# Three versions of the expert stage behind one branch on the token counts, in a fused attention, expert and feed-forward kernel

## The chip, the core and the metric

One core of a Trainium2 chip runs the whole program in one launch. The metric is device time in microseconds (us), the median over executions. TensorE (PE in the rows, PEld its weight loads), VectorE (DVE), ScalarE (ACT), GpSimd (POOL) and SyncE (SP) each work through a queue of their own, in order; a letter q behind an engine's name (PEldq, POOLq) marks what its sequencer does alone: register loads, branches, semaphores.

## The reference, cut to what matters

```python
# attention: q, k, v of 4 x 8 x 576 x 64; a row keeps its 32 largest scores, softmax, times v
x = attn_out as (2304, 512)
expert_idx = argmax(normalised x @ normalised expert_emb.T / tau)     # 8 experts
for e in range(8):                                                    # each token goes to one expert
    mask = expert_idx == e
    out[mask] = gate_w[mask] * (relu(x[mask] @ w1[e]) @ w2[e])        # 512 -> 1024 -> 512
h = out @ w_in                                                        # 512 -> 2048
return (max(h, 0) + alpha * min(h, 0)) @ w_out                        # 2048 -> 512
```

How many tokens an expert gets is known only when the router has run. The inputs are drawn by the reference itself with its default seed.

## The kernel before, in words

The program has three stages: attention with the router in its gaps, the expert stage, and the feed-forward stage (`last_products`). The router sorts tokens by expert into a DRAM buffer `xs` and ranks the experts: rank 0 is the expert that led after three of four batches, ranks 1 to 7 follow by size. The expert stage cannot have loops of a length found at run time, so each rank is computed over a fixed number of columns (tokens), `CAPS = (472, 408, 360, 328, 304, 296, 280, 256)`; columns beyond the expert's count are filled with rows that are thrown away. Two flags (`ro.flag`, L847 to L851) tell that a count went over its cap; in that case a branch at the end (L1842) redoes the rest, or all of it, in slow general code.

`Experts.run` (L1157) writes the stage out. It goes over nine blocks of columns: rank 0 in two (216 and 256 columns, blocks 0 and 1), then ranks 1 to 7 in one each (blocks 2 to 8). A block has two halves. In the first half each of 8 hidden tiles `f` takes 4 x 3 matmuls of n columns (L1108 to L1110: the numbers are split in a high and a low part, and three products are added), then ACT writes the high part (L1203) and DVE the low part (L1204). In the second half each of 4 output chunks `dc` takes 8 x 3 matmuls, and ACT or DVE copies it out of PSUM to `y` (L1246, L1248), from where SP stores it to the DRAM buffer `yt` (L1249). So a block is 192 matmuls of n columns. Between the chunks PE turns the next block's rows (`x_chunk`, L1100, one transpose for each 96 to 128 rows and each of 4 chunks). Weights come 8 units of 512 KB for an expert; SP fetches them (L921) into four buffers `raw`, and ACT and DVE or POOL split each in two halves (L1032, L1033) into one of 12 places. `tick` hands out these steps, and those of the feed-forward weights, by the list `plan`: a rank's first four units are split in the first half of the block before, its other four in the second half. Each engine's queue is in the order of the program text.

The feed-forward stage follows at the same pace on PE, then the last indirect stores of POOL (L1369), then every engine loads the flag word `redo` (L1840) and branches over the general code (L1842); each waits at semaphores that stand for what the skipped code would have counted.

Names that the steps below use: `ranks` (L816), `flags` and `redo` (L1140, L1149; a PE matmul L1152 sums the flags over partitions), `load_rows` (L1067), `load_columns` (L1260), `plan` (L1166), `stores` (L1249).

Of the kernel before, what the change touches and what calls it, by code (L numbers as in the profile page):

```python
# [502 lines left out]
CAPS = (472, 408, 360, 328, 304, 296, 280, 256)  # L503
FIRST = 216
XW = DM + 2
AHEAD = 3
# [10 lines left out]
class Router:  # L517
# [298 lines left out]
    def ranks(self):  # L816
# [6 lines left out]
        rank, first, t1 = self.rev, self.base, gt  # L823
        self.excess, self.over = key, gt[:, 0, 0:1]
        r3 = lambda a: a[:, None, :].to_broadcast([P, E, E])
        c3 = lambda a: a[:, :, None].to_broadcast([P, E, E])
# [25 lines left out]


def wide_words(nc, wk, raw, bufs):


    n = raw.shape[1] // 2
    v = raw.rearrange("p (f w) -> p f w", w=2)
    low, high = v[:, :, 0], v[:, :, 1]
    a = wk.tile([P, n], I32, name="wa", bufs=bufs)  # L860
    nc.vector.tensor_scalar(a, high, 3, 0x3FFFFFF8, op0=OP.logical_shift_left, op1=OP.bitwise_and)
    nc.vector.scalar_tensor_tensor(a, high, -0x40000000, a, op0=OP.bitwise_and, op1=OP.bitwise_or)
    nc.vector.tensor_scalar(high, a, -0x800000, None, op0=OP.bitwise_and)
# [5 lines left out]
SLOTS, EARLY, STAY = 12, 6, 8  # L869

LASTS = (0, 1, 2, 3, 8, 9, 10, 11, 4, 5, 6, 7, 12, 13, 14, 15)
# [14 lines left out]
class Experts:  # L886
# [3 lines left out]
    def __init__(self, tc, w1, w2, w_in, w_out, wa, xp, ident, xs, yt, idc, yp, ro, out):  # L890
        self.tc, self.nc = tc, tc.nc
        self.w1, self.w2, self.w_in, self.w_out = w1, w2, w_in, w_out
        self.ident, self.xs, self.yt, self.idc, self.out = ident, xs, yt, idc, out
        self.ro, self.wa, self.xp, self.yp = ro, wa, xp, yp
        self.W, self.rv = {}, {}
        self.items, self.sent = [], 0
        self.h0, self.p0, self.behind, self.ahead_of = [], [], [], []
        self.columns, self.numbers = None, []

# [23 lines left out]
    def unit(self, k):  # L923
        pool, n = (self.wa, EARLY) if k % SLOTS < EARLY else (self.wb, SLOTS - EARLY)
        return pool.tile([P, 2, 1024], F32R, name="wt", bufs=n)

# [23 lines left out]
    def plain(self, k):  # L950
        st = {}

        def load():
            st["r"] = self.wk.tile([P, 1024], F32, name="raw", bufs=4)
            self.fetch(st["r"], k)
        return load, lambda: self.split(k, st["r"])

    def wide(self, u, i):


        st, nc = {}, self.nc
        cs = slice(i * 512, (i + 1) * 512)

        def load():
            st["r"] = self.wk.tile([P, 1024], I32, name="raw", bufs=4)
# [42 lines left out]
    def first_blocks(self):  # L1008

        raws, v, nothing = {}, self.nc.vector, lambda: None  # L1010

        def add(j, m):
            def f():
                if not raws:
                    raws.update((i, self.wk.tile([P, 4, G2], F32, name="raw", bufs=4)) for i in (5, 6, 7, 4))
                self.sums(raws.get)[j][1]()
            return f
# [49 lines left out]
    def load_rows(self, r, o, n):  # L1067
# [4 lines left out]
        e, base = self.rv[r]  # L1072
        x = self.xp.tile([P, 4, XW], F32, name="xr")
        ld = nc.sync.dma_start(x[:p, :nj], self.xs[ds(e * NT + o, p * nj)].rearrange("(j p) d -> p j d", p=p))
# [19 lines left out]
    def x_chunk(self, rows, n, d, pt=None):  # L1094
# [4 lines left out]
        for j in range(nj):  # L1099
            nc.tensor.transpose(pt[:, j * p:(j + 1) * p], x[:p, j, d * P:(d + 1) * P], self.ident[:p, :p])  # L1100
        t = self.xp.tile([P, 2, MAXN], F32R, name="xT", bufs=4)
        nc.scalar.activation(t[:, 0, :n], pt[:, :n], AF.Copy)
# [46 lines left out]
    def redo(self, ones, f):  # L1149
# [4 lines left out]
        nc.vector.tensor_copy(n, pt[:, 0:2])  # L1154
        nc.vector.scalar_tensor_tensor(self.ro.redo, n[:, 0:1], 256.0, n[:, 1:2], op0=OP.mult, op1=OP.add)

    def run(self, ctx, alpha):  # L1157
# [9 lines left out]
        for r in range(1, E):  # L1167
            plan += [units(r + 1, 0), units(r + 1, 1)]
        blocks_of, none = self.first_blocks()
        plan[-2] += [self.last(d) for d in range(4)]  # L1170
# [13 lines left out]
        self.send(4)  # L1184
        rki = self.ro.rki
        ranks = self.ro.ranks()
# [4 lines left out]
        self.alpha = self.wk.tile([P, FF2 // P], F32, name="alpha")  # L1191
        nc.sync.dma_start(self.alpha, alpha.rearrange("(f p) -> p f", p=P))
        xT = self.x0
        for i, (r, o, n) in enumerate(blocks):
            nb = blocks[i + 1] if i + 1 < len(blocks) else None
            hT, nx = ([] if i else self.h0), []
            self.n = len(plan[2 * i])
            for f in range(8):
# [8 lines left out]
                if i == 0:  # L1207
# [4 lines left out]
                    if len(ranks) < 14 and 1 not in self.rv:  # L1212
                        registers()
                        rows = [self.load_rows(*nb)]
                if f >= GAT and nb and i:
                    self.gate(rows[0], f - GAT)
# [4 lines left out]
            if not nb:  # L1221
                nx = self.halves(rows[0])
            if i == 1:
                fl = self.flags()
            if i == 2:
                self.redo(*fl)
            base = self.rv[r][1]
            self.n = len(plan[2 * i + 1])

            def turn(at):  # L1230
                if nb:
                    nx.extend([self.x_chunk(rows[0], nb[2], d) for d in (XAT if i else XAT0)[at]])
# [24 lines left out]
            xT, rows = nx, rows[1:]  # L1257
        self.last_products(xT, len(plan[-2]), len(plan[-1]))

    def load_columns(self, g):  # L1260

        x = self.columns
        if x is None:
            x = self.columns = self.xp.tile([P, 4, XW], F32, name="xr")
        if g * G2 < NT:
# [8 lines left out]
    def halves(self, x):  # L1274
        out = []
        for d in range(4):
            t = self.xp.tile([P, 2, MAXN], F32R, name="xT", bufs=4)
            self.nc.scalar.activation(t[:, 0, :G2], x[:, d, :G2], AF.Copy)
# [4 lines left out]
    def last_products(self, t, n0, n1):  # L1283
# [133 lines left out]
        def new_sum(j):  # L1417
            if not raws:
                raws.update((i, self.wk.tile([P, 4, G2], F32, name="raw", bufs=4)) for i in (5, 6, 4, 7))
            self.sums(raws.get)[j][1]()  # L1420
# [75 lines left out]
        for m in (1, 6, 7, 5, 4, 2, 3):  # L1496
            product(k, m)


# [263 lines left out]
def tile_kernel(ctx, tc, q, k, v, emb, tau, w1, w2, w_in, w_out, alpha, out):  # L1763
# [11 lines left out]
    with ExitStack() as c0:  # L1775
# [95 lines left out]
```

## Time and profile before

| what | value |
|---|---|
| median of 3 runs (lowest, highest) | 1115.79 us (1114.88, 1116.54) |
| the profiled execution: its time | 1116.8 us |
| the profiled execution: its span, first to last instruction | 1115.1 us |
| mean granted TensorE clock | 0.998 |
| busy: PE, DVE, POOL, ACT | 96%, 78%, 67%, 65% |
| attention and router, up to the first matmul of rank 0's second block | 486.9 us |
| expert stage from there on (blocks 1 to 8) | 227.5 us |
| feed-forward stage, to the end of the span | 400.7 us |

The sum of a change is made against the profiled execution, which stands 1.0 us above the median of the runs; the 1.7 us between its time and its span lie around the first and last instruction. A stage is read from the stretch that it takes, since the shares of the whole span mix stages with different limits.

### The profile page before, as it was taken

What the parts mean: (1) busy time and instruction counts of PE and PEld (TensorE: products, weight loads), DVE (VectorE), ACT (ScalarE), POOL (GpSimd) and SP (SyncE); (2) the same over time, 40 slices, a digit from 0 to 9 for tenths busy, and PEclk for the clock granted to TensorE, in tenths of its full rate; (3) what the DMA queues carried; (4) which work ended last, traced back from release to release, by engine and by line L of the source; (5) the groups of instructions that cost most, each with busy time, mean ns of one, the idle gap of its engine ahead of it and who ended that gap; (6) DMA issues with size and microseconds to landing.
All of it is one profiled execution on the core that took longest, in us unless ns stands there. A gap on an engine that the chain in (4) does not pass through costs nothing. (4 is left out here: it accounts for less than half of the span.)

```text
span 1115.1 us, 27488 instructions
## 1 busy us (share of the span) xinstructions
PE 1068.7 (96%) x9529; PEld 1016.9 (91%) x9529; DVE 871.0 (78%) x3441; ACT 727.8 (65%) x1549; POOL 750.5 (67%) x790
## 2 busy tenths in 40 slices
PE   6999999999999998999999999999999999999996
PEld 4888889888887887999999999999999999999996
DVE  6999999999999999745456567787899978466554
ACT  6999999999999989645345555453434355433441
POOL 6999988888988888424435444255656695664674
PEclk9999999999999999999999999999999999999999
DMA  7456333443343324267567777146646122212301
GB/s 180 130 150 153 96 94 99 108 124 99 90 114 99 67 53 174 61 205 249 195 207 225 222 244 232 39 86 111 101 115 139 39 63 78 90 57 67 124 21 41
DMA packets 149531, 134.99 MB, mean 121 GB/s; under 512 B 95054, under 2 KB 117582, under 8 KB 149382
## 3 DMA queue, kind: packets, MB, share of 16 engines
q1 hardware_dynamic: 145334, 123.01, 41.0%
q0 software_dynamic: 2912, 9.46, 2.3%
q8 instruction: 77, 1.26, 0.5%
q10 hardware_dynamic: 1136, 0.67, 0.2%
q14 instruction: 72, 0.59, 0.2%
HBM read 89.82 MB, written 33.92 MB: 111 GB/s over the span
## 5 line engine op out<-in xcount | busy, mean ns | idle before, releaser
L1108 PE MATMUL mm<-xT,wt 128*128 128x256 f32 (+7 forms) x852 | 245.8, 288 | 2.1 <-DVE y L1382 2.1
L1109 PE MATMUL mm<-xT,wt 128*128 128x256 f32 (+7 forms) x852 | 246.3, 289 | 0.8 <-DVE xT L1279 0.8
L1110 PE MATMUL mm<-xT,wt 128*128 128x256 f32 (+7 forms) x852 | 245.5, 288 | 0.0
L297 POOL TENSOR_TENSOR sg<-ss,sg 128x576 f32<-128x576 f32 x143 | 201.7, 1412 | 32.0 <-ACT sg L286 30.2
L211 DVE MAX8 cand<-ss 128x8 f32<-128x96 f32 x864 | 210.8, 245 | 8.2 <-ACT ss L201 7.5
L1381 PE MATMUL mm<-wt,hT 128*128 128x256 f32 x1512 | 193.6, 282 | 1.1 <-DVE y L1382 0.9
L1381 PEld LDWEIGHTS mm<-wt,hT 128*128 128x128 f32 x1512 | 184.9, 189 | 2.2 <-issue 1.1
L1108 PEld LDWEIGHTS mm<-xT,wt 128*128 128x128 f32 x852 | 160.7, 189 | 3.0 <-DVE y L1382 2.7
L1109 PEld LDWEIGHTS mm<-xT,wt 128*128 128x128 f32 x852 | 160.8, 189 | 1.2 <-DVE xT L1279 1.2
L1110 PEld LDWEIGHTS mm<-xT,wt 128*128 128x128 f32 x852 | 160.9, 189 | 0.0
L970 POOL TENSOR_TENSOR wf<-wa,raw 128x512 f32<-128x512 f32 x32 | 48.8, 1524 | 117.2 <-DVE raw L865 83.2
L286 ACT ACTIVATE sg<-ss,w 128x576 f32<-128x576 f32 x144 | 118.3, 822 | 4.6 <-DVE w L224 4.0
L291 ACT ACTIVATE e<-ss,sm 128x576 f32<-128x576 f32 x144 | 117.6, 817 | 0.0
L322 PE MATMUL pt<-ident,e 128*128 128x128 f32 x576 | 114.9, 280 | 0.3 <-ACT pT L342 0.2
L323 PE MATMUL pt<-away,pen 128*128 128x128 bf16 x576 | 106.0, 220 | 2.7 <-POOL pen L306 2.7
L1033 POOL TENSOR_TENSOR wt<-raw,wt 128x1024 fp32r<-128x1024 f32 x28 | 68.5, 2447 | 58.5 <-ACT wt L1032 58.3
L233 DVE MAX8 w<-sg 128x8 f32<-128x576 f32 x144 | 106.5, 740 | 0.0
L189 PE MATMUL s<-kt,qq 64*128 64x144 f32 (+1 forms) x1280 | 100.3, 310 | 5.4 <-ACT pb L345 2.3
L201 ACT ACTIVATE ss<-s 128x576 f32<-128x576 f32 x144 | 100.2, 696 | 5.1 <-PE s L189 3.0
L189 PEld LDWEIGHTS s<-kt,qq 64*128 64x128 f32 (+1 forms) x1280 | 78.9, 183 | 22.1 <-issue 7.7
L356 PE MATMUL po<-va,pT 128*128 128x65 f32 (+1 forms) x640 | 86.6, 278 | 8.1 <-ACT pc L391 8.1
L342 ACT ACTIVATE pT<-pt 128x512 f32<-128x512 f32 x144 | 91.8, 637 | 0.8 <-PE pt L323 0.8
(295 smaller groups left out, 2731.2 us busy)
## 6 DMA issues: line engine op xcount, KB each, us to landing
raw<-in_moe_w SPq DMA_DIRECT2D x59, 512.0 KB
xr<-yt SPq DMA_DIRECT2D x17, 512.0 KB
qq<-qt SPq DMA_DIRECT2D x60, 144.0 KB
xs<-zeros SPq DMA_DIRECT2D x8, 1028.0 KB
raw<-in_moe_w_in SPq DMA_DIRECT2D x16, 512.0 KB
raw<-in_moe_w_out SPq DMA_DIRECT2D x16, 512.0 KB
yt<-zeros SPq DMA_DIRECT2D x8, 704.0 KB
rows<-in_q SPq DMA_DIRECT2D x32, 144.0 KB
```

The costliest lines, as they stand in the source:

```text
L189: nc.tensor.matmul(s[to, g, c * n:c * n + n], t["qq"][of, h, q0:q0 + m], t["k"][of, h * HALF + c * n:h * HALF + c * n + n], start=True, st ...
L211: blocks.append(lambda i=i: nc.vector.max(A.cand[:, i], A.ss[:, i * BW:(i + 1) * BW if i + 1 < KB else S]))
L233: fin = [lambda: nc.vector.max(C.w[:, 24:32], C.z), lambda: nc.vector.scalar_tensor_tensor(scr, self.vsel, C.c1, C.w[:, 23:32, None].to_br ...
L286: nc.scalar.activation(T.sg, T.ss, AF.Sign, bias=T.w[:, 23:24], scale=-ABOVE, accum_out=T.c1)
L291: nc.scalar.activation(T.e[:, self.place(T)], T.ss, AF.Exp, bias=T.sm[:, 0:1], scale=0.125)
L297: eng.tensor_tensor(T.z, T.ss, T.sg, op=OP.mult)
L322: nc.tensor.matmul(o, T.e[:, k:k + P], self.ident, is_transpose=True, start=True, stop=False)
L323: nc.tensor.matmul(o, T.pen[:, k:k + P], self.away, start=False, stop=True)
L1108: nc.tensor.matmul(ps, wh, xh, start=first, stop=False)
L1109: nc.tensor.matmul(ps, wh, xl, start=False, stop=False)
L1110: nc.tensor.matmul(ps, wl, xh, start=False, stop=last)
L1381: nc.tensor.matmul(ps, a[:, x, c], b[:, y, c], start=c == r == 0, stop=c == 3 and r == 2)
```

## The change

Block 1 is the last that all versions share. Behind it a branch on a word `wider`, which DVE computes from the counts, chooses among three versions of blocks 2 to 8 and of the whole feed-forward stage, which differ in the columns for ranks 1 to 7. The first version listed under the branch is `FLAT` or, by a second branch, `CAPS`; `STEEP` stands last. Python writes all that follows three times, from the same state. Tiles that live across the branch are named for their place and kept (`held`, `turn_of`) and no longer rotate. The jump to `STEEP` and the jump over the general code have a hint, which is placed some instructions ahead on all five engines.

```diff
+STEEP = (472, 400, 352, 320, 280, 256, 240, 240)
+FLAT = (472, 352, 336, 304, 288, 280, 256, 248)
...
+    def narrow_blocks(self):
+        v, x = self.nc.vector, self.beyond
+        self.wider = self.rki[:, 1, 0:2]
+        return [lambda a=a, r=r, c=c: v.tensor_scalar(x[:, a, r - 1:r], self.rank[:, r:r + 1], -float(c), None, op0=OP.add)
+                for a, caps in enumerate((STEEP, FLAT)) for r, c in enumerate(caps) if r] + [
+            lambda: v.tensor_reduce(x[:, 2, 0:2], x[:, 0:2, 0:E - 1], axis=AX.X, op=OP.max),
+            lambda: v.tensor_scalar(x[:, 2, 0:2], x[:, 2, 0:2], 0.0, None, op0=OP.max)]
...
+        over = self.ro.beyond[:, 2, 0:2]
+        nc.vector.scalar_tensor_tensor(self.ro.wider, n[:, 0:1].to_broadcast([P, 2]), 256.0, over, op0=OP.mult, op1=OP.max)
...
+        plan[4].insert(0, plan[3].pop())
...
+        xT, rows = self.blocks(blocks, plan, (0, 1), self.x0, [])
+        load = lambda a: nc.values_load(ro.wider[0:1, a:a + 1], min_val=0, max_val=256 * P + NT,
...
+        for _, f in self.stores:
+            f()
+        self.stores.clear()
...
+        def rest(caps):
...
+            narrow = blocks[:2] + [(r, 0, caps[r]) for r in range(1, E)]
+            t, _ = self.blocks(narrow, plan, range(2, len(blocks)), xT, list(rows))
+            self.last_products(t, len(plan[-2]), len(plan[-1]))
+        with tc.If(load(0) > 0, preferred_fallthrough_block=True, label="narrow") as wider:
+            with tc.If(load(1) == 0, preferred_fallthrough_block=True) as flat:
+                rest(FLAT)
+            with flat.Else():
+                rest(CAPS)
+        with wider.Else():
+            rest(STEEP)
...
+                if i == 1 and f in (2, 3):
+                    for step in self.narrow[8 * f - 16:8 * f - 8]:
+                        step()
+                    if f == 2:
+                        fl = self.flags()
+                if i == 1 and f == 4:
+                    self.redo(*fl)
...
-            if i == 1:
-                fl = self.flags()
-            if i == 2:
-                self.redo(*fl)
...
             for dc in range(4):
+                if i == 1 and dc == 2:
+                    self.tc.mark_branch_hint_location("narrow", "LikelyTaken", ENGINES)
...
         for m in (1, 6, 7, 5, 4, 2, 3):
             product(k, m)
+            if m == 7:
+                self.tc.mark_branch_hint_location("redo", "LikelyTaken", ENGINES)
...
-    with tc.If(again > 0):
+    with tc.If(again <= 0, preferred_fallthrough_block=False, label="redo") as usual:
+        pass
+    with usual.Else():
```

## Rows read from the trace of the kernel before

**Rows 1.** The page, busy time of TensorE over the whole span.

```profile
PE 1068.7 (96%) x9529; PEld 1016.9 (91%) x9529; DVE 871.0 (78%) x3441; ACT 727.8 (65%) x1549; POOL 750.5 (67%) x790
```

**Rows 2.** Block stretches: us; busy PE, PEld, DVE, ACT, POOL; clock; DMA share; GB/s.

```profile
511.37:548.29 36.92, 36.92 (x207) 36.63 (x206) 17.77 (x28) 15.76 (x25) 15.74 (x8) 1.00 0.61 201
548.29:580.95 32.66, 32.66 (x205) 32.61 (x205) 17.41 (x26) 15.49 (x25) 12.57 (x6) 1.00 0.62 199
580.95:611.03 30.08, 30.08 (x205) 30.06 (x205) 19.64 (x30) 15.38 (x25) 14.79 (x8) 1.00 0.74 235
611.03:639.03 28.00, 28.00 (x207) 28.00 (x206) 16.65 (x26) 14.80 (x25) 12.68 (x7) 1.00 0.75 232
639.03:666.13 27.10, 27.10 (x207) 27.10 (x205) 16.57 (x26) 14.66 (x25) 12.87 (x7) 1.00 0.76 238
666.13:691.76 25.63, 25.63 (x202) 25.63 (x201) 20.11 (x29) 13.24 (x24) 11.97 (x6) 1.00 0.79 254
691.76:714.44 22.68, 22.68 (x194) 22.68 (x193) 16.98 (x23) 11.43 (x21) 8.61 (x4) 1.00 0.14 49
```

**Rows 3.** Timeline of TensorE: first matmuls of half blocks; start and duration in us.

```profile
666.13 0.29 PE L1108 MATMUL mm<-xT,wt 128*128 128x280 f32 x1
...
678.55 0.29 PE L1108 MATMUL mm<-hT,wt 128*128 128x280 f32 x1
...
691.76 0.28 PE L1108 MATMUL mm<-xT,wt 128*128 128x256 f32 x1
...
703.07 0.28 PE L1108 MATMUL mm<-hT,wt 128*128 128x256 f32 x1
```

**Rows 4.** The same timeline in block 0: two matmuls of 216 columns, ten steps apart.

```profile
467.30 0.28 PE L1109 MATMUL mm<-xT,wt 128*128 128x216 f32 x1
...
468.42 0.27 PE L1110 MATMUL mm<-xT,wt 128*128 128x216 f32 x1
```

**Rows 5.** Lines L1840 and L1842, the register load and branch: ns, then first start.

```profile
L1840 PEldq TENSOR_LOAD <-redo x1: 486/486/486, 1102.6 to 1102.6; - x1
...
L1842 POOLq EVENT_SEMAPHORE  x6: 17/30/43, 1108.9 to 1110.0; - x6
L1842 ACTq EVENT_SEMAPHORE  x2: 17/17/17, 1100.0 to 1100.1; - x2
...
L1842 SPq COMPARE_BRANCH  x1: 53/53/53, 1053.3 to 1053.3; - x1
L1842 ACTq COMPARE_BRANCH  x1: 50/50/50, 1097.2 to 1097.2; - x1
L1842 PEldq COMPARE_BRANCH  x1: 3415/3415/3415, 1103.2 to 1103.2; - x1
...
L1842 POOLq INC_SWDGE_SEM  x1: 944/944/944, 1110.1 to 1110.1; - x1
```

**Rows 6.** The chain that ended last, its last sum: start, us, what.

```profile
1104.93 0.44 DVE y L1382
```

**Rows 7.** Line L1369, the indirect stores of the result: issue to landing.

```profile
L1369 POOL DMA_INDIRECT out<-y,idi x2: 973/974/974, 1103.3 to 1105.6; - x2
...
DMA to landing us min/median/max: 2.7/2.8/4.1
```

**Rows 8.** DMA queues between 1104 and 1112 us: packets, MB, share.

```profile
q14 instruction: 5, 0.04, 1.7%
q8 instruction: 2, 0.03, 1.6%
```

**Rows 9.** DVE's one-column operations of L844, ns, and what ACT waited for (510 to 715).

```profile
L844 DVE TENSOR_SCALAR key<-rev x8: 144/146/148, 475.3 to 475.7; 128x1 f32<-128x1 f32 x8
...
ACT y L1246 <- DMA yt<-y: 17.6, 5, 5.5
...
ACT wt L1032 <- DMA raw<-in_moe_w: 7.9, 4, 4.3
```

**Rows 10.** Timeline of ACT: the split of the last expert's last weight unit.

```profile
694.16 1.05 ACT L1032 ACTIVATE wt<-raw 128x1024 fp32r<-128x1024 f32 x1
```

More of the change, by code (lines that the diff above doesn't have):

```diff
@@ L824, in ranks @@
         self.excess, self.over = key, gt[:, 0, 0:1]
+        self.rank, self.beyond = rank, t0
         r3 = lambda a: a[:, None, :].to_broadcast([P, E, E])
@@ L869 @@
 SLOTS, EARLY, STAY = 12, 6, 8
+LOOSE = range(3, 8)
+ENGINES = tuple(getattr(mybir.EngineType, e) for e in ("PE", "DVE", "Activation", "Pool", "SP"))
 LASTS = (0, 1, 2, 3, 8, 9, 10, 11, 4, 5, 6, 7, 12, 13, 14, 15)
@@ L894, in __init__ @@
         self.ro, self.wa, self.xp, self.yp = ro, wa, xp, yp
-        self.W, self.rv = {}, {}
+        self.W, self.rv, self.places, self.turns = {}, {}, {}, {}
         self.items, self.sent = [], 0
         self.h0, self.p0, self.behind, self.ahead_of = [], [], [], []
-        self.columns, self.numbers = None, []
+        self.columns, self.numbers, self.fresh = None, [], {}
     def reg(self, ap, n):
@@ L923, in unit, with held, turn_of, raw @@
     def unit(self, k):
-        pool, n = (self.wa, EARLY) if k % SLOTS < EARLY else (self.wb, SLOTS - EARLY)
-        return pool.tile([P, 2, 1024], F32R, name="wt", bufs=n)
+        at = k % SLOTS
+        if at in LOOSE:
+            self.places.pop(("wt", at), None)
+        return self.held(self.wa if at < EARLY else self.wb, [P, 2, 1024], F32R, "wt", at)
+    def held(self, pool, shape, dtype, name, at):
+        if (name, at) not in self.places:
+            self.places[name, at] = pool.tile(shape, dtype, name=f"{name}{at}")
+        return self.places[name, at]
+    def turn_of(self, pool, shape, dtype, name, n):
+        at = self.turns.get(name, 0)
+        self.turns[name] = at + 1
+        return self.held(pool, shape, dtype, name, at % n)
+    def raw(self):
+        return self.turn_of(self.wk, [P, 1024], F32, "raw", 4)
     def split(self, k, raw):
@@ L953, in load @@
         def load():
-            st["r"] = self.wk.tile([P, 1024], F32, name="raw", bufs=4)
+            st["r"] = self.raw()
             self.fetch(st["r"], k)
@@ L964, in load @@
         def load():
-            st["r"] = self.wk.tile([P, 1024], I32, name="raw", bufs=4)
+            st["r"] = self.raw().bitcast(I32)
             nc.sync.dma_start(st["r"], self.wide_src(LASTS[u], i))
@@ L1008, in first_blocks @@
     def first_blocks(self):
-        raws, v, nothing = {}, self.nc.vector, lambda: None
+        raws, v, nothing = self.fresh, self.nc.vector, lambda: None
         def add(j, m):
@@ L1014, in f @@
                 if not raws:
-                    raws.update((i, self.wk.tile([P, 4, G2], F32, name="raw", bufs=4)) for i in (5, 6, 7, 4))
+                    raws.update((i, self.raw().rearrange("p (a b) -> p a b", a=4)) for i in (5, 6, 7, 4))
                 self.sums(raws.get)[j][1]()
@@ L1072, in load_rows @@
         e, base = self.rv[r]
-        x = self.xp.tile([P, 4, XW], F32, name="xr")
+        x = self.turn_of(self.xp, [P, 4, XW], F32, "xr", 1)
         ld = nc.sync.dma_start(x[:p, :nj], self.xs[ds(e * NT + o, p * nj)].rearrange("(j p) d -> p j d", p=p))
@@ L1100, in x_chunk @@
             nc.tensor.transpose(pt[:, j * p:(j + 1) * p], x[:p, j, d * P:(d + 1) * P], self.ident[:p, :p])
-        t = self.xp.tile([P, 2, MAXN], F32R, name="xT", bufs=4)
+        t = self.turn_of(self.xp, [P, 2, MAXN], F32R, "xT", 4)
         nc.scalar.activation(t[:, 0, :n], pt[:, :n], AF.Copy)
@@ L1184, in run, with blocks @@
         self.send(4)
-        rki = self.ro.rki
-        ranks = self.ro.ranks()
+        ro = self.ro
+        ranks = ro.ranks()
+        self.alpha = self.wk.tile([P, FF2 // P], F32, name="alpha")
+        nc.sync.dma_start(self.alpha, alpha.rearrange("(f p) -> p f", p=P))
+        self.ranks, self.narrow = ranks, ro.narrow_blocks()
+        xT, rows = self.blocks(blocks, plan, (0, 1), self.x0, [])
+        load = lambda a: nc.values_load(ro.wider[0:1, a:a + 1], min_val=0, max_val=256 * P + NT,
+                                        skip_runtime_bounds_check_because="a difference of counts or a sum of flags")
+        for _, f in self.stores:
+            f()
+        self.stores.clear()
+        mutable = ("turns", "V", "B", "stores", "behind", "ahead_of", "numbers", "W")
+        kept = {a: getattr(self, a).copy() for a in mutable}
+        kept.update((a, getattr(self, a)) for a in ("done", "sent", "step", "columns", "n"))
+        def rest(caps):
+            for a, x in kept.items():
+                setattr(self, a, x.copy() if a in mutable else x)
+            self.fresh.clear()
+            narrow = blocks[:2] + [(r, 0, caps[r]) for r in range(1, E)]
[8 more added lines that the diff above has]
+            rest(STEEP)
+    def blocks(self, blocks, plan, which, xT, rows):
+        nc, ro, ranks = self.nc, self.ro, self.ranks
+        rki = ro.rki
         def registers():
@@ L1190, in registers @@
                 self.rv[r] = (self.reg(rki[0:1, 0, r:r + 1], E - 1), self.reg(rki[0:1, 1, r:r + 1], NT))
[L1191 to L1194, printed above, removed]
+        for i in which:
+            r, o, n = blocks[i]
             nb = blocks[i + 1] if i + 1 < len(blocks) else None
@@ L1257, in run @@
             xT, rows = nx, rows[1:]
-        self.last_products(xT, len(plan[-2]), len(plan[-1]))
+        return xT, rows
     def load_columns(self, g):
@@ L1263, in load_columns @@
         if x is None:
-            x = self.columns = self.xp.tile([P, 4, XW], F32, name="xr")
+            x = self.columns = self.turn_of(self.xp, [P, 4, XW], F32, "xr", 1)
         if g * G2 < NT:
@@ L1276, in halves @@
         for d in range(4):
-            t = self.xp.tile([P, 2, MAXN], F32R, name="xT", bufs=4)
+            t = self.turn_of(self.xp, [P, 2, MAXN], F32R, "xT", 4)
             self.nc.scalar.activation(t[:, 0, :G2], x[:, d, :G2], AF.Copy)
@@ L1418, in new_sum @@
             if not raws:
-                raws.update((i, self.wk.tile([P, 4, G2], F32, name="raw", bufs=4)) for i in (5, 6, 4, 7))
+                raws.update((i, self.raw().rearrange("p (a b) -> p a b", a=4)) for i in (5, 6, 4, 7))
             self.sums(raws.get)[j][1]()
```

## The prediction

> **What bounds the kernel now.** I read the page first: PE is busy for 96% of the span, so a stage gets shorter only where PE's own work does [rows 1]. The change touches the expert stage, so next I cut that stage at the first matmul of each block. [...] The blocks are 408, 360, 328, 304, 296, 280 and 256 columns wide. Last I read the branch at the end, the only jump that this program takes [rows 5], and the chain of work that ended last there [rows 6].
>
> **Which version runs.** I worked the router's counts out from the reference on the inputs it draws: 404 tokens for rank 0, then 377, 338, 261, 246, 232, 226 and 220. STEEP allows 400, 352, 320, 280, 256, 240 and 240, so all fit, the tightest (338 in 352, 226 in 240) by 14 tokens. FLAT would not take them, as 377 is over 352. The branch therefore takes the jump that has the hint, to the version that stands last.
>
> **Narrower blocks.** From 408 to 360 columns a block falls from 36.92 to 32.66 us, 0.089 us a column; from 360 to 328 by 0.081; from 328 to 304 by 0.087 [rows 2]. Ranks 1, 2 and 3 each lose 8 columns: 0.71 + 0.64 + 0.69 = 2.04 us. Rank 4 goes from 304 to 280, and the block of 280 columns stands in the trace (with the two transposes a chunk that it will have too): 28.00 - 25.63 = 2.37 us [rows 2].
>
> Rank 5 goes from 296 to 256. A half block without transposes is 96 matmuls: 678.55 - 666.13 = 12.42 us at 280 columns, 0.1294 us each, and 703.07 - 691.76 = 11.31 us at 256, 0.1178 us each [rows 3]. A block of 256 in the middle of the stage is thus 25.63 - 192 x 0.0116 = 23.4 us, and 27.10 - 23.4 = 3.7 us go.
>
> Ranks 6 and 7 get 240 columns, a width that the trace does not have. Ten steps at 216 columns take 1.12 us, 0.112 each [rows 4]. From 280 to 256 the step fell by 0.48 ns a column, as at the wide blocks (0.089 us / 192 = 0.46 ns), so 256 still lies on that slope, which would put 216 at 0.099. The row is 13 ns above it, so something other than columns holds the step there; 16 columns below 256 the slope is at 0.110, already under the level of 216. So 240 is near that level: I take 0.113. Rank 6 then saves 192 x (0.1294 - 0.113) = 3.15 us, rank 7 192 x (0.1178 - 0.113) = 0.92 us. The ends are 0.112 (3.34 and 1.11) and 0.1178, no better than 256 (2.23 and 0).
>
> [...]
>
> Sum of the blocks: 2.04 + 2.37 + 3.7 + 3.15 + 0.92 = 12.2 us, between 10.4 and 12.6.
>
> **What must keep up.** Per expert the other engines do the same steps in less time. DVE has 20.11 us of work in the block of 280 columns, which shrinks to about 22.5 us; it stays under it, as its share for hidden tiles shrinks as well [rows 2]. Transfers are 254 GB/s at a share of 0.79 there [rows 2]: the same bytes in 22.5 us ask for 289 GB/s at 0.90. ACT has waited for weights four times in the stage, 7.9 us together [rows 9], but the last unit of the last expert is split by ACT at 694.16 and its half block begins at 703.07 [rows 3, 10]: some 8 us of cover. I take nothing for it; the price without cover is a rival below.
>
> **The branch itself.** DVE gets 16 small operations and one more that forms the word: the eight of L844 start within 0.4 us of each other and last 146 ns each [rows 9], so about 1.3 us, in block 1, where PE has several free PSUM banks. The flags' matmul, moved to the fifth hidden tile, waits for a DVE cast queued behind half of them: at most 0.5 us on PE, I take 0. At the branch each engine loads the word (486 ns on PE [rows 5]) and compares. PE's sequencer runs ahead of its array: at the end it loaded the flag at 1102.6, while the last product came out at 1104.9 [rows 5, 6]. That lead of 2.3 us covers load and compare if the jump costs nothing more. Without a hint it costs more: on ACT 2.8 us pass from the branch (1097.2) to the next instruction (1100.0), on PE the branch lasts 3.4 us [rows 5]. Then PE is idle from 1104.9 to 1106.6 in the picture of the end: 1.7 us. The hint stands half a half block ahead, 48 matmuls of 256 columns or 5.7 us, more than 3.4. I take 0.2 us, with ends 0 and 1.9.
>
> [...]
>
> The rest at the branch: SP sends the last store of block 1 before it branches and not a tick later; ACT's copy for such a store has waited up to 5.5 us for an earlier store [rows 9], so SP may hold some weight fetches back by 2 to 3 us. Behind SP's wait stand only fetches with many us of cover; ACT and DVE lose below 1 us each, and PE has two free banks. One weight split moves from the end of block 1 to the start of block 2, still half a block before its use. The kept tiles come round in the same order as the rotating ones. All this I cost at 0.
>
> **The end.** The last POOL store starts at 1105.6, behind DVE's last sum, and the landing of these stores takes 2.8 us in the median and 4.1 at most [rows 6, 7]. The instruction queues move seven packets in that window [rows 8]: code fetched for the jumps, on the engines that carry the store. POOL's semaphores behind the jump stand from 1108.9 to 1110.0 [rows 5]; a landing 4.1 us behind 1105.6 is at 1109.7, so the late landing, not the jump, ends last. With the fetches moved to the hint, 5.7 us earlier, up to 4.1 - 2.8 = 1.3 us go; I take 1.0, ends 0 and 1.3. Against it, where three versions meet again their semaphores must agree. They issue the same transfers, so I take 0.2 us; if POOL had to do a second set behind the landing (1108.9 to 1111.0 [rows 5]), 2.0 us.
>
> **Sum.** 12.2 - 0.2 + 1.0 - 0.2 = 12.8 us off 1116.8 gives 1104.0 for an execution like the profiled one, and off the median 1103.0.
>
> **Rivals.**
> - *The hint is not obeyed*, or its code is pushed out before the jump. Blocks as above, the branch costs 1.7 to 1.9, the end gains nothing: 12.2 - 1.8 - 0.2 = 10.2, 1105.6. For it: the trace shows no hinted jump, and PE runs some 100 instructions between hint and jump.
> - *Entering and leaving a version makes engines wait for each other.* PE would wait at the branch for ACT's late copy (3 us) and start again from an empty queue (2 us), and POOL would do its second set at the end (2.0): 12.2 - 7 = 5.2, 1110.6. Against it: at the old branch each engine goes on alone, SP at 1053, ACT at 1097, PE at 1103 [rows 5].
> - *Weights come late.* If fetches cannot go faster than in the block of 280, the last three blocks give back what they gain beyond the cover, some 3 us: 1106.
> - *Slower: the wide version runs.* This decides if a count is over its STEEP cap, at the word's load behind block 1. No column is saved. PE pays the outer load, the code that the hint put in the wrong place (3.4), a second load (0.5) and the unhinted inner jump (3.4): 0.5 + 3.4 + 0.5 + 3.4 - 2.3 of lead = 5.5, less 0.8 at the end: 1120.5. Against it stand the counts, with 14 tokens to spare.
>
> **Chances.** Forecast 0.62, hint not obeyed 0.18, waits at the joints 0.08, late weights 0.07, wide version 0.05. With every term at its better end 13.9 us go (1101.9), with the blocks and the branch at their worse ends 8.5 (1107.3); some 0.9 us for the spread of the runs comes off the lower end. So 1101.0 to 1107.3 holds the forecast, the missed hint and late weights, and leaves out the joints and the wide version, 0.13, and a little of the others. About 0.2% (2.2 us) is what a measurement of this kernel can tell from no change. All cases but the last are faster by more than that, except the joints at their worst: faster 0.92, same 0.03, slower 0.05.
>
> **What would show it.** Stretches from block to block of about 36.2, 32.0, 29.4, 25.6, 23.4, 22.5 and 21.7 us with PE busy throughout; matmuls 240 columns wide with steps of 0.113 us; no PE gap at the first matmul of 400 columns, and less than 1 us between an engine's compare and its next instruction; the last store landing in 2.8 us. Matmuls of 408 columns would show the wide version; a gap of 1.5 us or more before the first of 400 columns would show a hint that does not work.

## The result and the profile after

The changed kernel takes 1103.57 us in the median (1102.83 to 1105.30, 6 executions) against 1116.16 us (1114.88 to 1120.77, 6 executions): a ratio of 0.9881, 95% interval 0.9864 to 0.9897: 12.6 us less. The forecast was 1103.0, 12.8 us less. The profiled execution took 1103.42 us with a span of 1101.7, where before had 1115.1.

The page, busy time by engine: PE has 13.1 us less to do than in [rows 1], at the same share.

```profile
PE 1055.6 (96%) x9521; PEld 1003.6 (91%) x9521; DVE 875.2 (79%) x3458; ACT 725.7 (66%) x1547; POOL 752.6 (68%) x790
```

The stretches from block to block for ranks 1 to 7, columns as in [rows 2]:

```profile
511.29:547.47 36.18, 36.18 (x206) 36.09 (x205) 18.11 (x27) 16.61 (x26) 15.51 (x7) 1.00 0.66 201
547.47:579.57 32.10, 32.10 (x206) 32.06 (x205) 17.32 (x26) 15.35 (x25) 12.55 (x6) 1.00 0.63 199
579.57:608.83 29.26, 29.26 (x206) 29.25 (x205) 19.55 (x30) 15.23 (x25) 14.72 (x8) 1.00 0.71 236
608.83:634.25 25.42, 25.42 (x202) 25.42 (x201) 16.23 (x26) 13.88 (x24) 12.33 (x7) 1.00 0.77 251
634.25:657.96 23.71, 23.71 (x203) 23.71 (x201) 16.56 (x26) 13.84 (x24) 12.99 (x6) 1.00 0.79 266
657.96:680.64 22.68, 22.68 (x202) 22.50 (x201) 18.13 (x25) 12.65 (x23) 13.16 (x7) 1.00 0.80 266
680.64:702.78 22.14, 22.11 (x194) 21.73 (x193) 18.70 (x27) 11.12 (x21) 9.66 (x4) 1.00 0.21 67
```

PE is busy for all but 0.03 us of these stretches, and each block is shorter than its row in [rows 2]: by 0.74, 0.56, 0.82, 2.58, 3.39, 2.95 and 0.54 us, 11.6 together. The second thing to see is DVE: in the last two blocks 18 to 19 us of work now stand beside 22, and in the last one PEld (21.73) has come apart from the stretch (22.14).

Timeline of PE at the branch and in the last block (start, duration):

```profile
511.17 0.28 PE L1140 MATMUL mm<-hT,wt 128*128 128x256 f32 x1
511.29 0.35 PE L1138 MATMUL mm<-xT,wt 128*128 128x400 f32 x1
...
682.10 0.28 PE L1139 MATMUL mm<-xT,wt 128*128 128x240 f32 x1
...
683.22 0.28 PE L1140 MATMUL mm<-xT,wt 128*128 128x240 f32 x1
```

The first matmul of 400 columns follows the last of 256 at the usual step of 0.12 us: the branch leaves no gap. Ten steps at 240 columns take 1.12 us, the level that [rows 4] showed at 216.

The branch (L1240), the hints (booked on L1939), the jump at the end (L1912) and the last store (L1437): ns, then first and last start.

```profile
L1240 PEldq COMPARE_BRANCH  x1: 402/402/402, 509.8 to 509.8; - x1
L1240 ACTq COMPARE_BRANCH  x1: 73/73/73, 515.5 to 515.5; - x1
...
L1939 ACTq BRANCH_PREFETCH_HINT  x2: 31/38/45, 0.8 to 516.0; - x2
L1939 PEldq BRANCH_PREFETCH_HINT  x2: 40/43/46, 0.9 to 510.2; - x2
...
L1912 POOLq EVENT_SEMAPHORE  x6: 17/30/43, 1093.6 to 1096.5; - x6
L1912 PEldq COMPARE_BRANCH  x2: 200/280/361, 1090.5 to 1092.6; - x2
L1912 POOLq INC_SWDGE_SEM  x1: 947/947/947, 1096.6 to 1096.6; - x1
...
L1437 POOL DMA_INDIRECT out<-y,idi x2: 969/970/970, 1090.5 to 1092.9; - x2
```

PE's branches last 0.4 us where the one of [rows 5] lasted 3.4. The hints did not run where the text places them: each of the five engines ran one in the first microsecond of the program and the other as the first thing behind the branch. At the end POOL's counter follows the start of the last store by 3.7 us, where it was 4.5 (1105.6 to 1110.1 [rows 5, 7]).

Where the span went, worked out from the first matmuls of the blocks and the last sum of DVE in each profile (us):

| kernel | start of block 1 | block 1 | ranks 1 to 7 | feed-forward, to the last sum | rest | span |
|---|---|---|---|---|---|---|
| before | 486.9 | 24.5 | 203.1 | 390.9 | 9.7 | 1115.1 |
| after | 486.7 | 24.6 | 191.5 | 389.9 | 9.1 | 1101.7 |
| after, again | 486.8 | 24.6 | 191.6 | 389.7 | 8.9 | 1101.6 |
| one narrow version | 488.3 | 24.7 | 192.7 | 389.8 | 10.7 | 1106.1 |
| same widths in all versions | 486.6 | 24.6 | 202.9 | 389.8 | 8.9 | 1112.8 |
| no hint at the branch | 486.6 | 27.3 | 191.4 | 389.7 | 9.3 | 1104.2 |
| no hint at the end | 486.7 | 24.6 | 192.4 | 389.7 | 11.4 | 1104.8 |
| wide version by a wrong hint | 489.4 | 30.9 | 204.4 | 391.6 | 11.1 | 1127.3 |
| narrow version first | 488.2 | 24.6 | 194.6 | 389.7 | 12.0 | 1109.1 |
| tight widths | 486.6 | 24.6 | 190.1 | 389.7 | 8.9 | 1099.9 |
| tight, y in four halves | 492.4 | 24.6 | 186.9 | 389.8 | 8.9 | 1102.6 |
| tight, half the weights | 488.0 | 24.6 | 180.7 | 390.4 | 8.9 | 1092.6 |
| after, y in four halves | 488.4 | 24.6 | 194.6 | 389.9 | 8.9 | 1106.3 |
| tight, no POOL in the last splits | 486.2 | 24.6 | 184.2 | 389.8 | 9.2 | 1094.0 |

Of the change only the first hint lies in the first column; it differs by up to 6 us between profiles, and is taken out of what follows.

### The profile page after: what moved, and what is told of

It is laid out like the page before. It is cut to its first block, busy times and chain, and to the rows that moved or that the text cites. A ratio compares the mean times of both kernels' runs of the same rounds, so it can differ in the third digit from the quotient of the medians.

```text
span 1101.7 us, 27452 instructions
## 1 busy us (share of the span) xinstructions
PE 1055.6 (96%) x9521; PEld 1003.6 (91%) x9521; DVE 875.2 (79%) x3458; ACT 725.7 (66%) x1547; POOL 752.6 (68%) x790
## 5 line engine op out<-in xcount | busy, mean ns | idle before, releaser
L1138 PE MATMUL mm<-xT,wt 128*128 128x256 f32 (+6 forms) x852 | 243.7, 286 | 1.2 <-DVE y L1450 1.0
L1139 PE MATMUL mm<-xT,wt 128*128 128x256 f32 (+6 forms) x852 | 244.0, 286 | 0.9 <-DVE xT L1347 0.8
L1140 PE MATMUL mm<-xT,wt 128*128 128x256 f32 (+6 forms) x852 | 243.3, 286 | 0.0
```

Source lines behind the costliest of these rows:

```text
L1138: nc.tensor.matmul(ps, wh, xh, start=first, stop=False)
L1139: nc.tensor.matmul(ps, wh, xl, start=False, stop=False)
L1140: nc.tensor.matmul(ps, wl, xh, start=False, stop=last)
```

## The experiments: where the gain is

**One narrow version, no branch** (the kernel before with other `CAPS`):

```diff
-CAPS = (472, 408, 360, 328, 304, 296, 280, 256)
+CAPS = (472, 400, 352, 320, 280, 256, 240, 240)
```

> The kernel before with the narrow widths written in as its only version: the columns alone, no branch behind block 1, no hint at the end. If the gain is the columns and the branch costs PE nothing, the seven blocks take the 191.5 us that they take in the changed kernel, and the time is 11.6 us below before (12.6 if the wait of 1.05 us in the feed-forward stage goes as well). If the branch takes something that the trace hides, this kernel is faster than the changed one, by 0.5 us or more.

Measured: 1107.27 us (1104.03 to 1113.10), ratio 0.9927 (0.9909 to 0.9946).

**All versions with the widths of before** (branch, hints and kept tiles only):

```diff
-STEEP = (472, 400, 352, 320, 280, 256, 240, 240)
+STEEP = (472, 408, 360, 328, 304, 296, 280, 256)
```

> The changed kernel with the wide widths in the version that runs: branch, hints and kept tiles alone, no column saved. If the branch is free, PE has no gap at the first matmul behind it, the seven blocks take 203.1 us as before, and the time is 0.6 us (the end) to 1.7 us (with the wait in the feed-forward stage) below before. If the branch costs something, it is above before by that: 1.9 us for a jump that is not prefetched.

Measured: 1114.82 us (1113.80 to 1119.30), ratio 0.9999 (0.9987 to 1.0010). Its block 1 and its ranks 1 to 7 take 24.6 and 202.9 us, where before had 24.5 and 203.1. So the branch and what comes with it cost nothing that can be measured, and the widths are the gain. The single version should then be as fast as the changed kernel and was not. Its profile shows why in part: 1.6 us ahead of the stage, 1.6 us at the end, where it has no hint, and 1.2 us in the blocks. The feed-forward stage is 1.1 us shorter in both than in the profile of before, so neither the branch nor the new widths are needed for that.

## The experiments: the hints

**No hint at the branch**:

```diff
-                if i == 1 and dc == 2:
-                    self.tc.mark_branch_hint_location("narrow", "LikelyTaken", ENGINES)
...
-        with tc.If(load(0) > 0, preferred_fallthrough_block=True, label="narrow") as wider:
+        with tc.If(load(0) > 0, preferred_fallthrough_block=True) as wider:
```

> The changed kernel without the hint for the jump behind block 1. If the hint is what makes this jump cheap, 2.8 to 3.4 us pass on every engine from its compare to its next instruction, and PE, whose lead is 2.1 us, stands still for 1.5 to 2.0 us before the first matmul of 400 columns: 1.7 us above the changed kernel. If the lead or the kept code hides the jump anyway, there is no gap and the times agree within 0.5 us.

Measured: 1111.25 us (1106.05 to 1116.48), ratio 0.9963 (0.9941 to 0.9985). The timeline of PE at the branch, in the fastest of its executions:

```profile
511.05 0.28 PE L1140 MATMUL mm<-hT,wt 128*128 128x256 f32 x1
513.90 0.44 PE L1138 MATMUL mm<-xT,wt 128*128 128x400 f32 x1 [2.58 <-ACT y L1312]
```

The gap is 2.7 us wider than with the hint, more than the 1.9 that the prediction had as its worse end. The other executions took up to 10 us longer, and the median stands 7.7 us above the changed kernel where 1.7 was expected; no profile shows where the rest went.

**No hint at the end**:

```diff
-            if m == 7:
-                self.tc.mark_branch_hint_location("redo", "LikelyTaken", ENGINES)
...
-    with tc.If(again <= 0, preferred_fallthrough_block=False, label="redo") as usual:
+    with tc.If(again <= 0, preferred_fallthrough_block=False) as usual:
```

> The changed kernel without the hint for the jump over the general code at the end. If the late landing of the last store and not the jump ends last, POOL's compare is followed by its next instruction after 2.8 us instead of 0.4, the last store lands in about 4.1 us instead of 3.4, and the time is 0.6 us above the changed kernel (up to 1.3). If the hint gives nothing, the two agree within 0.3 us.

Measured: 1107.04 us (1106.52 to 1109.71), ratio 0.9933 (0.9916 to 0.9950). The jump at the end and the last store, as above:

```profile
L1910 PEldq COMPARE_BRANCH  x2: 187/1836/3484, 1091.2 to 1095.1; - x2
L1910 POOLq INC_SWDGE_SEM  x1: 947/947/947, 1099.7 to 1099.7; - x1
...
L1437 POOL DMA_INDIRECT out<-y,idi x2: 973/973/973, 1091.3 to 1093.6; - x2
```

PE's jump is back at 3.5 us, and from the last store to POOL's counter 6.1 us pass and not 3.7. By the table's column of the rest, the profiles of kernels without this hint (before, one narrow version, this one) have 9.7, 10.7 and 11.4 us behind the last sum, mean 10.6; the nine with the hint, where no other jump stands between, have 8.9 to 9.3, mean 9.0. The hint is worth some 1.6 us, between 0.4 and 2.5 by these profiles. This kernel's median is 3.5 us above the changed one's, more than the 1.3 expected at most; in the profiles 2.3 us of it are at the end and 0.9 in the blocks.

**The wide version, against the hint** (`STEEP` too narrow for rank 1):

```diff
-STEEP = (472, 400, 352, 320, 280, 256, 240, 240)
+STEEP = (472, 368, 352, 320, 280, 256, 240, 240)
```

> STEEP allows rank 1 only 368 columns, and 377 tokens come: the outer jump is not taken against its hint, the inner one is taken without a hint, and the version with the widths of before runs. The prediction's slower rival priced this at 5.5 us on PE, 4.7 over the kernel before: 1120.5. Theory 'every change of place that no hint announced costs a fetch' : two gaps on PE of 2 to 3 us each behind block 1, so 1114.8 (the same widths with a hint that was right) + 4 to 6 = 1119 to 1121. Rival 'a jump that falls through costs nothing whatever the hint said': one gap of 2.9 us, 1117.5 to 1118.

Measured: 1125.02 us (1119.93 to 1134.54), ratio 1.0071 (1.0039 to 1.0103). The outer and the inner branch on PE; behind them the timeline of PE; and stretches with columns as in [rows 2]:

```profile
L1240 PEldq COMPARE_BRANCH  x1: 104/104/104, 513.9 to 513.9; - x1
...
L1241 PEldq COMPARE_BRANCH  x1: 5574/5574/5574, 514.5 to 514.5; - x1
```

```profile
520.25 0.70 PE L1138 MATMUL mm<-xT,wt 128*128 128x408 f32 x1 [4.80 <-issue]
```

```profile
520.25:523.20 2.95, 2.95 (x9) 2.87 (x10) 0.00 (x0) 0.00 (x0) 0.71 (x1) 0.50 0.19 65
```

Falling through against the hint takes 0.1 us (104 ns). The inner jump, taken without a hint, costs PE 5.6 us while the DMA share is 0.87, and behind that idle stretch PE is granted 0.50 of its clock for its first 3 us. Block 1 is 6.3 us longer than with the same widths and a right hint, rank 1's block 1.5 us. So the fall-through was cheap although the hint said otherwise, as the rival had it, but both expectations of the time (1117.5 to 1121) were too low for the median.

**The narrow version first**, reached by falling through, without a hint at the branch:

```diff
-        with tc.If(load(0) > 0, preferred_fallthrough_block=True, label="narrow") as wider:
-            with tc.If(load(1) == 0, preferred_fallthrough_block=True) as flat:
-                rest(FLAT)
-            with flat.Else():
-                rest(CAPS)
-        with wider.Else():
-            rest(STEEP)
+        with tc.If(load(0) <= 0, preferred_fallthrough_block=True) as narrow:
+            rest(STEEP)
+        with narrow.Else():
...
```

> The narrow version stands first, so that the branch falls through to it, and there is no hint for it. Theory 'only a taken jump needs a hint': no gap on PE at the branch; the jump over the other two versions comes only at the end of the narrow one, where DVE, POOL and SP would pay it: 1103.5 to 1106. Rival 'a branch costs its fetch in any case without a hint': a gap of 2.5 to 3 us, as in the version without the hint, and 1106 to 1107.

Measured: 1110.31 us (1109.01 to 1115.66), ratio 0.9954 (0.9924 to 0.9985). Lines of the branch with its way out (L1240) and of the jump at the end (L1910):

```profile
L1240 PEldq COMPARE_BRANCH  x2: 95/1781/3467, 511.3 to 1094.5; - x2
...
L1910 PEldq COMPARE_BRANCH  x2: 202/1500/2797, 1098.4 to 1101.6; - x2
```

At the branch nothing is lost (95 ns). The price comes at the end: the way out over the other two versions lasts 3.5 us, and the jump behind it 2.8 in spite of its hint. The rest behind the last sum is 12.0 us in place of 9.1. Standing last is therefore worth 2.9 us to the narrow version. The theory held at this branch, only the taken jump needs the hint (4.1 us on PE without it, against these 95 ns), but 1110.31 lies above both expectations. What else this kernel lost (3.1 us in the blocks) is the next question.

## The experiments: what the narrow blocks wait for

**The changed kernel again**, on the same chip as the wide version, the narrow version first and the tight widths:

> The changed kernel itself, once more, because the kernels with its narrow widths (one version of the stage, or one hint taken away) spread over 5 to 10 us from execution to execution where the kernel before spreads over 2. Theory 'the narrow blocks are near what the transfers can bring, and some executions pay': this one spreads as well, between 1103 and 1108, and the slow ones show PE waiting for DVE in the blocks of ranks 6 and 7. Rival 'kept tiles are what keeps it tight' (the single version has the rotating tiles): between 1102.8 and 1105.3, as it was first measured, and no such wait.

Measured: 1104.15 us (1103.41 to 1108.46), ratio 0.9904 (0.9870 to 0.9937), blocks as in the changed kernel's first profile. Three of its four executions lie within 1.1 us and one 4 us above them, which parts the two expectations poorly; the profile has no wait of PE worth a row.

In the narrow version that stood first the last block took 25.33 us, not 22.14. Timelines of DVE, POOL and PE there:

```profile
690.51 3.32 DVE L1063 TENSOR_TENSOR wt<-wf,wt 128x1024 fp32r<-128x1024 f32 x1
693.76 1.34 DVE L1267 SCALAR_TENSOR_TENSOR hT<-mm,hT 128x240 fp32r<-128x240 f32 x4
695.02 3.18 DVE L1063 TENSOR_TENSOR wt<-wf,wt 128x1024 fp32r<-128x1024 f32 x1
```

```profile
690.36 2.39 POOL L1063 TENSOR_TENSOR wt<-wf,wt 128x1024 fp32r<-128x1024 f32 x1 [1.49 <-ACT wt L1062]
694.72 2.38 POOL L1063 TENSOR_TENSOR wt<-wf,wt 128x1024 fp32r<-128x1024 f32 x1 [1.97 <-ACT wt L1062]
```

```profile
694.21 0.38 PE L1138 MATMUL mm<-hT,wt 128*128 128x240 f32 x1 [0.92 <-DVE hT L1267]
698.56 0.38 PE L1139 MATMUL mm<-hT,wt 128*128 128x240 f32 x1 [1.95 <-DVE hT L1267]
```

And the first pair in the changed kernel, DVE and POOL:

```profile
689.07 1.21 DVE L1063 TENSOR_TENSOR wt<-wf,wt 128x1024 fp32r<-128x1024 f32 x1
```

```profile
689.17 3.37 POOL L1063 TENSOR_TENSOR wt<-wf,wt 128x1024 fp32r<-128x1024 f32 x1 [1.73 <-ACT wt L1062]
```

The two engines form the low parts of the first feed-forward weights. In these pairs whichever starts first has its own time (DVE 1.21, POOL 2.39), and the other ends as much later: POOL's 690.36 + 2.39 = 692.75, plus 1.2, is 693.95, and DVE's operation ends at 693.83. A start 0.1 us earlier or later decides here whether DVE loses 2.1 us, and behind it stand the hidden tiles that PE waits for. Why the second ends later is not shown; by how much is, to 0.1 us.

Whether that, late weights or late stores hold the narrow blocks was tried on narrower ones, the **tight widths**:

```diff
-STEEP = (472, 400, 352, 320, 280, 256, 240, 240)
+STEEP = (472, 384, 344, 264, 248, 232, 232, 224)
```

> STEEP as tight as these counts allow: 384, 344, 264, 248, 232, 232, 224. By the steps measured so far (0.46 ns a column above 256, a floor of 0.112 us a step at 240 and below): 1.4 + 0.7 + 4.9 + 2.2 + 1.1 + 0.1 + 0.1 = 10.5 us less than the changed kernel, 1093, if nothing else ends last. Theory 'the narrow blocks are near what the transfers can bring': four blocks in a row of some 22 us ask for 290 GB/s throughout, PE waits for DVE or ACT from the second of them on, and 2 to 6 us of the gain are lost: 1095 to 1099, with a spread of several us. If the floor is not a floor, the blocks at 232 and 224 get shorter than 21.6 us.

Measured: 1101.45 us (1098.13 to 1101.97), ratio 0.9858 (0.9826 to 0.9889): 2.1 us below the changed kernel where 10.5 were worked out, worse than either expectation. The blocks of ranks 4 and 7, columns as in [rows 2], and what ACT and PE waited for behind 580 us:

```profile
602.62:627.19 24.57, 23.24 (x202) 23.04 (x201) 18.58 (x28) 14.11 (x25) 14.12 (x7) 1.00 0.84 287
...
674.34:701.29 26.95, 23.84 (x194) 23.29 (x193) 21.03 (x27) 10.89 (x21) 8.45 (x4) 0.94 0.16 53
```

```profile
ACT wt L1062 <- DMA raw<-in_moe_w: 20.1, 19, 4.2
...
PE mm L1139 <- DVE hT L1267: 5.9, 4, 2.0
```

**Tight widths, y in four halves**:

```diff
+                if i > 1 and n <= 256 and len(self.pair) < 2:
+                    self.pair.append(self.wk.tile([P, 512], F32, name="y", bufs=2))
+                if i > 1 and n <= 256:
+                    y = self.pair[dc % 2][:, dc // 2 * 256:dc // 2 * 256 + 256]
```

> The tight widths again, and for blocks of 256 columns and less the two output tiles y, which hold 512 columns, are used as four halves: a copy out of PSUM then waits for a store issued four copies ago, not two. Theory 'ACT is held by the landing of its own stores, and the weight splits behind that copy come late': the waits of ACT for the landing of yt go (8.9 us behind 580 with two), PE's waits in the blocks of ranks 4 to 7 shrink to under 1 us each block, and the time falls from 1101.5 towards 1095. Rival 'the weights themselves land late': the copies no longer wait, but ACT waits for the weights as long or longer, PE's waits stay, and the time stays within 1.5 us of 1101.5.

Measured: 1101.99 us (1098.85 to 1104.78), ratio 0.9864 (0.9836 to 0.9891). No gain in the median. ACT's wait for the weights stays at 20.7 us behind 585, and PE's waits went from 7.0 to 4.3 us; the last block, in which DVE was first once, took 22.8 us.

**Tight widths, half the weights of ranks 3 to 7**:

```diff
+            h = 512 if 24 <= k < 64 else 1024
+            self.nc.sync.dma_start(raw[:, :h], s[:, :h])
...
+            raw = raw[:, :512].rearrange("p (a b) -> p a b", a=1).to_broadcast([P, 2, 512])
```

> The tight widths again, with half of each weight unit of ranks 3 to 7 left out: only its first half is fetched, and the split reads that half twice (so the products of these experts are with other weights). Conversions, products and stores are as many as before; 10 MB of transfers are gone. Theory 'the weights land late': the waits for weights go, the blocks take their matmuls' time (25.3 to 24.3, then 23.2, 21.6 to 22.0 three times), and the time is 1093 to 1095. Rival 'ACT is held by the landing of its stores': PE's waits stay at 5 us or more and the time at 1099 or above.

Measured: 1094.10 us (1093.57 to 1100.67), ratio 0.9819 (0.9785 to 0.9852), as worked out for blocks without waits. The same two blocks:

```profile
604.04:627.20 23.16, 23.16 (x203) 23.05 (x201) 16.54 (x27) 13.35 (x24) 14.78 (x7) 1.00 0.67 198
...
671.83:693.27 21.44, 21.44 (x195) 21.44 (x193) 19.61 (x27) 11.34 (x21) 10.41 (x4) 1.00 0.15 47
```

PE is busy throughout both. With earlier weights the operations of DVE and POOL also meet at other moments, so this run alone does not part the two causes.

**The changed kernel, y in four halves** (the edit of the run with tight widths):

> The changed kernel with the four halves of y in the blocks of 256 columns and less. If the landing of stores is what holds ACT at these widths, the last two blocks, 22.7 and 22.1 us, take 21.9 and 21.8 and the spread of the runs gets smaller: 1102.5. If not, 1103.5 to 1104.2, the same as the changed kernel.

Measured: 1107.21 us (1105.05 to 1108.74), ratio 0.9915 (0.9897 to 0.9933). More room for stores gains nothing: the time lies above both expectations. The last block took 25.30 us, and POOL was first in both pairs (DVE 3.2 and 3.3 us).

**Tight widths, no POOL in the last expert's feed-forward splits**:

```diff
-POOL, POOLV = (0, 2), (1, 3)
+POOL, POOLV = (0, 2), ()
```

> The tight widths once more, and the two of the last expert's four feed-forward splits whose low part POOL formed give it to DVE. In the profile of the tight widths DVE takes 3.27 and 3.26 us for such a low part when POOL has begun the same operation 0.2 us earlier (POOL 2.4 and 2.4), and 1.21 us when it began first. Theory 'DVE stands still until POOL's operation has ended, and behind it stand the hidden tiles that PE waits for': these four operations take 1.2 to 1.3 us each on DVE, PE's waits of 0.53, 1.12 and 2.27 us in the last block go, the block takes 22.3 to 23.3 us in place of 26.95, and the time is 1097.5 to 1098.5. Rival 'only the late weights hold the last block': it stays above 25.5 us, or gets longer by the 2.4 us of work that DVE has in addition, and the time is 1101 to 1104.

Measured: 1096.56 us (1095.77 to 1098.08), ratio 0.9825 (0.9811 to 0.9838), the fastest of the kernels that do all the work, 7 us below the changed one's 1103.57. (Its widths leave the counts of ranks 1 to 7 from 0 to 7 columns; other counts would take a wider version.) Blocks of ranks 4 and 7, then DVE's splits in the last one:

```profile
602.15:627.05 24.90, 23.20 (x202) 23.00 (x201) 18.91 (x27) 13.96 (x25) 13.92 (x8) 1.00 0.83 279
...
672.57:694.93 22.36, 21.95 (x194) 21.59 (x193) 18.53 (x29) 10.89 (x21) 3.67 (x2) 1.00 0.21 69
```

```profile
L1063 DVE TENSOR_TENSOR wt<-wf,wt x4: 1207/1208/1209, 681.2 to 686.4; 128x1024 fp32r<-128x1024 f32 x4
```

DVE has two operations more and 2.5 us less to do. The last block falls from 26.95 to 22.36 us: DVE's wait for POOL is shown there, 1.21 us a split in place of 3.27 and 3.26 (part of the 4.6 us is the clock, 0.94 in that stretch with tight widths and 1.00 here). Without POOL in the splits, the changed kernel itself was not run.

Rank 4's block stays at 24.90, against 23.16 with half the weights. Its one listed wait of PE, and the operations of DVE and POOL ahead of it:

```profile
614.10 1.32 POOL L1000 TENSOR_TENSOR wf<-wa,raw 128x512 f32<-128x512 f32 x1 [2.28 <-DVE raw L878]
```

```profile
614.27 2.23 DVE L1063 TENSOR_TENSOR wt<-raw,wt 128x1024 fp32r<-128x1024 f32 x1
```

```profile
616.88 0.38 PE L1139 MATMUL mm<-hT,wt 128*128 128x248 f32 x1 [1.70 <-DVE hT L1267]
```

The wait is here too, with another operation of POOL: DVE's split takes 1.0 us more than alone (2.23 for 1.21), and the hidden tiles behind it are what PE waits for. With half the weights the same split takes 2.24 us as well and PE does not wait, since it comes 10.3 us behind the start of the block and not 12.1. So in this block late transfers and DVE's wait for POOL add up. That the transfers are those of the weights is the likely reading (ACT waits 20.1 us for them in the tight widths, 9.3 in the changed kernel), but no run took DVE's wait for POOL alone out of this block.

## Why the prediction was right, step by step

**Blocks: right, 11.6 for 12.2.** By rank the working had 0.71, 0.64, 0.69, 2.37, 3.7, 3.15 and 0.92; measured are 0.74, 0.56, 0.82, 2.58, 3.39, 2.95 and 0.54. The level for 240 columns, the choice that carried ranks 6 and 7, was right: 0.112 us a step. It is a floor: the half blocks of 232 and 224 columns in the run with half the weights take 10.7 us as well, 0.112 a matmul. What is short is rank 7: 22.14 us for 192 x 0.112 = 21.5. The rest of 0.6 us stands almost wholly in two places, 688.89 and 694.00 us, where PE's steps are 0.2 to 0.3 us. At each, a split of DVE that took 2.33 or 2.17 us behind POOL's had just ended. The second, DVE and PE:

```profile
691.46 2.17 DVE L1063 TENSOR_TENSOR wt<-wf,wt 128x1024 fp32r<-128x1024 f32 x1
```

```profile
694.00 0.38 PE L1139 MATMUL mm<-hT,wt 128*128 128x240 f32 x1
```

So the price of a matmul held, and what the prediction put at nothing in this block was DVE's wait for POOL.

**What must keep up: the thin point.** The prediction compared DVE's busy time with the block and looked for cover of the weights. Both held in the profile on record, by little. What it did not ask is when DVE works: in the narrow version that stood first, two operations that each stand some 2 us behind POOL's made the last block 25.3 us long in place of 22.1. In the kernel before DVE was first too, and its block had 5.7 us of slack (16.98 of 22.68 [rows 2]). The rival of the late weights (0.07, 1106) did not happen at these widths; at the tight ones late transfers and DVE's wait for POOL together lengthen the block of rank 4.

**The branch: right in its sum (0 for 0.2), wrong in its working.** "The hint stands half a half block ahead, 48 matmuls of 256 columns or 5.7 us, more than 3.4" failed: it ran with the first instructions of the program, 509 us before its jump, as if moved to the start of the straight stretch of code that it is written in. It works all the same. The missed hint, a rival at 1105.6, was run for this jump alone: 1106.05 us in the profile and 1111.25 in the median. PE loses 2.7 us there and not 1.7; 0.7 of the difference is its branch, which lasts 4.1 us and not 3.4.

**The end: right in kind, 0.6 for 1.0 less 0.2.** The jump costs POOL little now, 0.4 us from its compare to its next instruction (1093.2 to 1093.6) where it was 2.9 (1106.0 to 1108.9), and what POOL waits for behind it still ends last (its semaphores stand until 1096.5), as the prediction said of the landing. The last store did not land at the median of [rows 7]; POOL's counter came 3.7 us behind its start. Over all profiles the hint is worth some 1.6 us, above the range given (0 to 1.3). That fetched code holds up the landing fits: three packets of the instruction queues move between 1090 and 1099 us with the hint, six between 1093 and 1104 us without it. No run parts it from the jump itself.

**Not in the sum, and luck:** 1.05 us of the feed-forward stage, waits for DVE in the one profile of before that are missing in the one of after and in most others. That they are an effect of the change is not shown; without them the sum of the profiles is 12.3 us. The medians agree with the forecast (12.6 for 12.8) better than the terms do, and the two medians of before, 1115.79 and 1116.16, lie 0.4 us apart.

**The range.** Its lower gain of 8.5 us is 10.4 - 1.9 with the end at nothing; with the end as forecast it is 9.3. The blocks at their worse end sum to 10.3 and not 10.4. Neither changes what the range holds.

**The rivals.** No waits at the joints appeared: the step from block 1 to rank 1 is as in a straight program. The wide version, forecast 4.7 us above before, was 9 us above when it was forced. The price of the inner jump was too low, 3.4 for 5.6 us, and the clock behind it was not thought of; the second price, for a hint that proves wrong, was too high (3.4 for 0.1).

What stays open: why three kernels with narrow blocks (one narrow version, no hint at the branch, narrow version first) spread over 7 to 10 us, and what moves the start of block 1. The granted clock goes with part of it. Without the hint at the branch, the six executions of 1110.5 us and more had a mean clock of 0.984 to 0.987, the four below 0.988 to 0.997; whether the clock is the cause there or follows from waits is not shown. And in the profile where block 1 starts latest, at 492.4 us, PE was granted 0.70 between 10 and 50 us, in the others 0.83 to 1.00; the starts at 488 to 489 us are not explained by that.

## What to carry to other kernels

The cost of a matmul followed the columns only down to a floor here, 0.112 us at 240 columns and below, and the rows of an already narrow stage (216 columns) showed it beforehand. When the bounding engine's stage is shortened, compare the second engine's order of work, not only its busy time, and above all where operations of VectorE and GpSimd overlap in time: here the last block took 25.3 us with POOL's subtractions first and 22.1 with DVE's first split ahead. A version chosen at run time was free here (ratio 0.9999 with the widths of before), standing last and with hints for both its jumps; of the other versions the wide one was run, and it cost 9 us more than the kernel before.

## What the runs showed of the hardware that was not expected

- A hint held for long: the one that PE ran at 510.2 us still served its jump at 1090.5 (0.36 us), and the one of 0.9 us the jump at 509.8 (0.40 us). With another taken jump in between, PE's hinted jump took 2.8 us again (narrow version first) and 3.1 (wide version).
- The price of a taken jump without a hint on PE was 3.4 and 3.5 us at the end, at a DMA share of 0.24 and 0.23 in these stretches, and 4.1 and 5.6 us in the expert stage, at 0.91 and 0.87. That the transfers make it dearer is not shown. A branch that falls through took 0.1 us with a wrong hint and without any.
- DVE's subtraction of 128x1024 took 1.21 us alone and up to 3.3 us behind POOL's, with a start 0.1 us apart deciding which.
